# Smaller first units, relays of their own rows, and loads of k, v and x in pieces, in an attention and feed-forward kernel

## The chip, the cores and the metric

One of the eight cores of a Trainium2 chip runs the whole program. A core has TensorE (PE, matrix products into PSUM), VectorE (DVE), ScalarE (ACT), GpSimd (POOL) and SyncE (SP). In this kernel SyncE does nothing but issue the DMA transfers, one after the other in the order of the program; sixteen DMA engines move the bytes. The metric is the device time of one execution in microseconds. The time before is the median of three runs.

## The reference

Four batches of twelve heads, 448 tokens of width 64. The scores of the twelve heads are mixed by a 12 by 12 matrix before the softmax, and the attention weights by another after it. Then comes a block that mixes tokens through rank 32 and channels through a hidden layer of 3072 with relu.

```python
scores = scale * np.matmul(q, k.transpose(0, 1, 3, 2))
scores = np.einsum('bhij,hg->bgij', scores, w_pre)
scores = scores - np.max(scores, axis=-1, keepdims=True)
attn = np.exp(scores)
attn = attn / (np.sum(attn, axis=-1, keepdims=True) + 1e-09)
attn = np.einsum('bhij,hg->bgij', attn, w_post)
x = np.matmul(attn, v)            # then to [B, S, H * D]
...
h = xt @ U @ V                    # xt is x with tokens last
u = x + h.transpose(0, 2, 1)
return u + np.maximum(u @ w_ch1, 0.0) @ w_ch2
```

## The kernel before, in words

The work on attention goes by chunks of ten query tokens: 45 chunks a batch, 180 in all. Chunks are grouped into units, four to a batch: `UNITS` (line 22) gives 12, 12, 12, 9 chunks for batches 0 and 2 and 11, 12, 12, 10 for batches 1 and 3.

For a unit, `load_q` (L384) fetches the query columns and, per batch, `load_k` (L380) the keys in three transfers of one, two and three pairs of heads. For each of the six pairs of heads `qk` (L397) makes scores on TensorE, for all rows of the unit at once, `qk_out` (L401, whose copies stand at L309 and L311) evicts them to a tile s, and two `relay` transfers (L404) carry them, one per head, to a tile t, where the heads lie on partitions, as the mixing needs. A relay moves ten partitions of twelve chunks whatever the unit has. There are two t tiles, used in turn by the units, and three s tiles.

Two chunks make one pair of the softmax part: `premix` (L428) mixes the heads and needs all twelve relays of its units, `neg_max` (L433) is the row maximum on VectorE, `exp` (L438) the exponential on ScalarE, `recip` (L445) and `scale_w` (L449) put the reciprocal of the sum into the second mixing matrix, `postmix` (L461) mixes the heads again on TensorE, and `post_out` evicts into a tile a. When a unit's chunks are done, `av` (L499) multiplies by v in two groups of three pairs of heads, and `store_x` (L508) writes the result to a scratch xs in device memory. `load_v` (L491) fetches the v of a batch in one transfer into a single buffer, so the v of the next batch waits for the last `av` of this one.

After attention, `load_x` (L667) reads a batch of xs back in one transfer into a tile acc; `flip` (L672) transposes, `by_u` (L690) and `by_v` (L703) apply the rank 32 matrices, and `up` (L743), `down` (L763) and `gather` (L767) are the hidden layer. Its weights come as 8-byte words (`load_raw`, L580), are made into floats on VectorE and GpSimd, and each is split into a high and a low part. Eight of these pieces are converted early, between the attention steps, and parked in device memory (L612, L616).

The order of all of this is computed when the program is built. Each step is given with its engine, a guessed cost, a rank, the steps that it needs and the buffers it takes; `Plan.order` plays the engines forward in time and lets each take the ready step of lowest rank whose buffers are free. The program is then written in that order, engine by engine. So the order of the transfers on SyncE is fixed, and a transfer that must wait holds up all behind it. Two lines decide much of it, the rank and cost of a relay and of a load:

```python
plan.add(("relay", u, h), [("SP", (1040, 1000))], partial(relay, u=u, h=h), r + RANK["qo"], [("qk_out", u, p)], [s, ("t", u)])
plan.add(("v", un.b), [("SP", (500, 6700))], partial(load_v, b=un.b), rank_av(u, 0) - RANK["vr"], (), [("vr", un.b)])
```

SyncE's transfers take eight completion semaphores in turn, DMAHW0 to DMAHW7 in the order, so a transfer waits until the one eight places before it has landed.

Of the kernel before, what the change touches and what calls it, by code (L numbers as in the profile page):

```python
# [21 lines left out]
UNITS = [[12, 12, 12, 9], [11, 12, 12, 10]] * 2  # L22
NG = 4
NJ = 4
# [19 lines left out]
class Unit:  # L44


    def __init__(self, b, gi):
        self.b, self.gi, self.n = b, gi, UNITS[b][gi]
        self.i0 = MC * sum(UNITS[b][:gi])
        self.rows = MC * self.n  # L50
        self.tokens = min(S, self.i0 + self.rows) - self.i0
# [5 lines left out]
    av_step=1.6, post=4.6, kr=6, vr=4, qr=9.129, mx=0.782, ex=1.2, ep=2.4, po=0.9, qo=0.4, rl=10.285,  # L57
# [202 lines left out]
def build(tc, q2, kt, vj, wpre_in, wpost_in, u_in, v_in, ident, w1j, w2, out, show=None):  # L260
# [5 lines left out]
    def pool(ctx, name, bufs, side="left", **kw):  # L266
# [4 lines left out]
        wr=3, e=3, st=4, a0=1, a1=1, a2=1, vr=1, x=2, kr=2, k=2, q=3, s=3, tmp1=1,  # L271
# [75 lines left out]
    units = [Unit(b, gi) for b in range(B) for gi in range(NG)]  # L347
# [34 lines left out]
    def load_q(eng, u, p, n, src):  # L382
        q = tile_of(("q", u), lambda: sb["q"].tile([128, H // 2, QW], F32, "q"))
        eng.dma_start(out=q[:, p:p + n], in_=src[:, p:p + n])  # L384
# [14 lines left out]
    def qk_out(eng, u, p):  # L399
        s = T["s", u, p] = sb["s"].tile([QW, 2, S], F32, "s")  # L400
        copy(eng, s, T.pop(("qk", u, p))[:QW, :, :S])  # L401

    def relay(eng, u, h):
        eng.dma_start(out=tt[u % 2][QA + h::H], in_=T["s", u, h // 2][QA:, h % 2])  # L404

    at = 0
    for u, un in enumerate(units):
        b, size = un.b, 128 * (H // 2) * QW
        src = q2[at:at + size].rearrange("(p h i) -> p h i", p=128, h=H // 2)
        at += size  # L410
        for p in range(0, H // 2, 3):
            plan.add(("q", u, p), [("SP", (430, 880))], partial(load_q, u=u, p=p, n=3, src=src), rank_qk(u, 2 * p) - RANK["qr"], (), [("q", u)])
        for p in range(H // 2):
            r = rank_qk(u, 2 * p)
            o, s = ("qk", (u, p)), ("s", (u, p))
            plan.add(("qk", u, p), [("PE", 760)], partial(qk, u=u, p=p), r, [("q", u, p // 3 * 3), ("k", b, (0, 1, 1, 3, 3, 3)[p])],
                     [o, ("q", u), ("k", b)])
            plan.add(("qk_out", u, p), OUT(2 * S), partial(qk_out, u=u, p=p), r + RANK["qo"], [("qk", u, p)], [o, s], port=())
            for h in (2 * p, 2 * p + 1):
                plan.add(("relay", u, h), [("SP", (1040, 1000))], partial(relay, u=u, h=h), r + RANK["qo"], [("qk_out", u, p)], [s, ("t", u)])  # L420
# [68 lines left out]
    def load_v(eng, b):  # L489
        v = T["v", b] = sb["vr"].tile([AP, H // 2, 2, NJ, D], F32, "v")  # L490
        eng.dma_start(out=v, in_=vj[b].rearrange("p (h i n d) -> p h i n d", h=H // 2, i=2, n=NJ))  # L491

    def av(eng, u, p):
        v, a, n = T["v", units[u].b], T["a", u], units[u].rows
        z = T["z", u, p] = bank("av", (u, p))[:, :AV * 120].rearrange("p (a n) -> p a n", a=AV)
        for c in range(AV):
            for jj in range(NJ):
                for i in range(2):
                    eng.matmul(z[i * D:(i + 1) * D, c, :n], lhsT=v[:, p + c, i, jj, :], rhs=a[:, jj * H + 2 * (p + c) + i, :n], start=(jj == 0), stop=(jj == NJ - 1))  # L499
# [10 lines left out]
    for u, un in enumerate(units):  # L510
        if un.gi == 0:
            plan.add(("v", un.b), [("SP", (500, 6700))], partial(load_v, b=un.b), rank_av(u, 0) - RANK["vr"], (), [("vr", un.b)])
        for p in range(0, H // 2, AV):
            r = rank_av(u, p)
            z, x = ("av", (u, p)), ("x", u)
            plan.add(("av", u, p), [("PE", 300 + AV * 816)], partial(av, u=u, p=p), r, [("v", un.b)] + [("post_out", c) for c in range(first[u], first[u + 1]) if ("post_out", c) in plan.steps],
                     [("vr", un.b), (f"a{u % 3}", u), z])
# [148 lines left out]
    def load_x(eng, b):  # L666
        eng.dma_start(out=acc[b], in_=xs[b].rearrange("c p s -> p c s"))  # L667
# [213 lines left out]
```

## Time and profile before

| | |
|---|---|
| median of 3 runs | 1167.31 us (1164.23 to 1170.02) |
| the profiled execution | 1160.33 us |
| its span in the profile | 1158.2 us, mean granted TensorE clock 0.979 |
| TensorE busy | 1086.0 us, 94% |
| VectorE, ScalarE, GpSimd busy | 730.3, 390.5 and 258.4 us |
| moved by DMA | 118.18 MB, mean 102 GB/s |
| attention, by the last postmix | up to about 380 us |

The profile page gives the busy time of each engine, the span in 40 slices with the granted clock (1.00 is full speed, 0.50 half) and the DMA rate, the chain of work that ended last, and the costliest groups of instructions. The trace behind it answers for single stretches, lines and tiles. Names such as t<-s mean "written from". TensorE's weight loads are a row of their own, PEld.

### The profile page before, as it was taken

Reading aid. Unit: us, or ns where it says so; the run is one execution under the profiler, and the core shown is the slowest. Engines: PE = TensorE matmul, PEld = TensorE weight load, DVE = VectorE, ACT = ScalarE, POOL = GpSimd, SP = SyncE. Lnnn points to the kernel's source line nnn. Section 1 sums busy time; section 2 is a strip of 40 time slices with the busy share of each in tenths; the row PEclk is TensorE's granted clock in tenths of the full one; section 3 lists DMA queues with packets and bytes.
Section 4 is the critical chain, followed back from the end, with each engine's and each line's share of the span. In section 5 each row is a group of like instructions: output and inputs, shape, how many; then the busy total and the mean of one; then the engine's idle time right before and its main releaser. Section 6 shows DMA issues by size and latency. Waiting matters only on the chain.

```text
span 1158.2 us, 29292 instructions
## 1 busy us (share of the span) xinstructions
PE 1086.0 (94%) x12456; PEld 902.0 (78%) x12456; DVE 730.3 (63%) x1271; ACT 390.5 (34%) x817; POOL 258.4 (22%) x389
## 2 busy tenths in 40 slices
PE   3799898989989879999999999999999999999998
PEld 0476565656657768898898989898989898989897
DVE  0554454545766775887676767676767676776634
ACT  2677565757666523322111111111111121212100
POOL 3111111111123332243122222221222222222100
PEclk7899999999999889999999999999999999999999
DMA  8556746656775710122111111111111121112004
GB/s 239 188 178 189 202 154 189 173 172 183 205 212 180 224 43 1 28 69 69 54 55 55 55 55 55 55 55 55 55 55 55 55 55 56 55 41 60 10 14 178
DMA packets 68030, 118.18 MB, mean 102 GB/s; under 512 B 17804, under 2 KB 54108, under 8 KB 67420
## 3 DMA queue, kind: packets, MB, share of 16 engines
q1 hardware_dynamic: 67900, 116.31, 33.9%
q8 instruction: 98, 1.61, 0.6%
q14 instruction: 32, 0.26, 0.1%
HBM read 62.72 MB, written 12.28 MB: 65 GB/s over the span
## 4 chain that ended last, share of the span: by engine, by line
PE 83%; DMA 7%; DVE 5%; issue 2%; ACT 2%; SPq 1%; POOL 0%; ACTq 0%; DVEq 0%; POOLq 0%
PE bank L743 30%; PE bank L763 29%; PE bank L461 6%; PE bank L499 6%; DMA t<-s 5%; PE bank L428 5%; PE bank L397 5%; PE bank L690 1%; DVE acc L767 1%; DMA v<-in_vj 1%; PE bank L672 1%; SPq L404 1%; DVE xl L316 1%; ACT s L309 1%; DVE a L599 1%
## 5 line engine op out<-in xcount | busy, mean ns | idle before, releaser
L767 DVE TENSOR_TENSOR acc<-acc,bank 128x448 f32<-128x448 f32 x300 | 183.9, 619 | 76.2 <-PE bank L763 71.2
L763 PE MATMUL bank<-hh,w1l 128*128 128x448 f32 x576 | 215.2, 374 | 1.7 <-DVE xl L316 0.6
L743 PE MATMUL bank<-uh,w0l 128*128 128x448 f32 x576 | 213.0, 370 | 0.9 <-DVE acc L706 0.7
L743 PE MATMUL bank<-ul,w0h 128*128 128x448 f32 x576 | 212.5, 369 | 0.0
L743 PE MATMUL bank<-uh,w0h 128*128 128x448 f32 x576 | 212.3, 369 | 0.0
L763 PE MATMUL bank<-hl,w1h 128*128 128x448 f32 x576 | 211.4, 367 | 0.0
L763 PE MATMUL bank<-hh,w1h 128*128 128x448 f32 x576 | 211.4, 367 | 0.0
L748 ACT ACTIVATE hh<-bank 128x448 fp32r<-128x448 f32 x96 | 52.3, 545 | 396.2 <-PE bank L743 364.1
L433 DVE TENSOR_REDUCE mx<-bank 128x2 f32<-128x896 f32 x90 | 97.7, 1087 | 109.7 <-PE bank L428 109.7
L608 POOL TENSOR_TENSOR a<-a,x 128x384 f32<-128x384 f32 (+2 forms) x99 | 100.2, 1012 | 292.1 <-DVE x L604 283.6
L461 PEld LDWEIGHTS bank<-wr,e 60*56 60x56 f32 (+1 forms) x5760 | 103.2, 133 | 57.6 <-issue 48.2
L752 DVE SCALAR_TENSOR_TENSOR hl<-bank,hh 128x448 fp32r<-128x448 f32 x96 | 59.8, 623 | 133.2 <-ACT hh L748 132.1
L763 PEld LDWEIGHTS bank<-hh,w1l 128*128 128x128 f32 x576 | 108.3, 188 | 22.0 <-DVE acc L767 9.7
L461 PE MATMUL bank<-wr,e 60*56 60x60 f32 (+1 forms) x5760 | 107.9, 220 | 16.8 <-issue 13.6
L397 PE MATMUL bank<-k,q 64*60 64x448 f32 (+1 forms) x768 | 101.0, 580 | 20.8 <-ACT s L309 13.6
L438 ACT ACTIVATE e<-bank,mx 128x448 f32<-128x448 f32 x180 | 112.7, 636 | 16.3 <-DVE rc L445 8.5
L743 PEld LDWEIGHTS bank<-uh,w0l 128*128 128x128 f32 x576 | 109.1, 189 | 11.6 <-DVE acc L706 1.0
L743 PEld LDWEIGHTS bank<-uh,w0h 128*128 128x128 f32 x576 | 108.9, 189 | 10.1
L743 PEld LDWEIGHTS bank<-ul,w0h 128*128 128x128 f32 x576 | 108.9, 189 | 9.9
L763 PEld LDWEIGHTS bank<-hh,w1h 128*128 128x128 f32 x576 | 108.3, 188 | 9.7
L763 PEld LDWEIGHTS bank<-hl,w1h 128*128 128x128 f32 x576 | 108.3, 188 | 9.0
L428 PE MATMUL bank<-t,wpre 64*64 64x448 f32 x720 | 92.8, 560 | 8.3 <-DMA t<-s 4.8
(59 smaller groups left out, 1147.3 us busy)
## 6 DMA issues: line engine op xcount, KB each, us to landing
t<-s SPq DMA_DIRECT2D x192, 210.0 KB
kr<-in_w1j SPq DMA_DIRECT2D x48, 384.0 KB
kr<-in_w SPq DMA_DIRECT2D x48, 384.0 KB
q<-in_q SPq DMA_DIRECT2D x32, 186.0 KB
v<-in_vj SPq DMA_DIRECT2D x4, 1440.0 KB
acc<-xs SPq DMA_DIRECT2D x4, 1344.0 KB
out<-acc SPq DMA_DIRECT2D x24, 224.0 KB
xs<-x SPq DMA_DIRECT2D x10, 360.0 KB
```

What stands on the lines that cost most here:

```text
L397: eng.matmul(o[at, i, :S], lhsT=q[d, p, at], rhs=k[d, p, :], start=True, stop=True)
L428: eng.matmul(o[64 * j:64 * j + 64, i, :S], lhsT=wpre[64 * i:min(64 * i + 64, QW)], rhs=tt[u % 2][64 * i:min(64 * i + 64, QW), n, :], start ...
L433: eng.tensor_reduce(out=mx, in_=T["pre", k][:, :, :S], axis=AX.X, op=ALU.max, negate=True)
L438: eng.activation(out=e[:, i], in_=T["pre", k][:, i, :S], func=ACTF.Exp, bias=T["mx", k][:, i:i + 1], accum_out=sm[:, i:i + 1])
L461: eng.matmul(d[:, jj * H:(jj + 1) * H, i], lhsT=e[64 * j:64 * j + HALF, i, j0:j0 + m], rhs=wr[64 * j:64 * j + HALF, i].rearrange("p (g m) ...
L499: eng.matmul(z[i * D:(i + 1) * D, c, :n], lhsT=v[:, p + c, i, jj, :], rhs=a[:, jj * H + 2 * (p + c) + i, :n], start=(jj == 0), stop=(jj == ...
L608: eng.tensor_tensor(out=f32(a), in0=f32(a), in1=f32(x), op=ALU.add)
L743: eng.matmul(ps, lhsT=w[:, c * 128:(c + 1) * 128], rhs=u[:, c, :], start=(i == 0), stop=(i == 3 * KC - 1))
L748: eng.activation(out=hh, in_=T["up", f, b], func=ACTF.Relu)
L752: eng.scalar_tensor_tensor(out=hl, in0=T.pop(("up", f, b)), scalar=0.0, in1=f32(T["hh", f, b]), op0=ALU.max, op1=ALU.subtract)
L763: eng.matmul(ps, lhsT=w[:, cut], rhs=h, start=(i == 0), stop=(i == len(todo) - 1))
L767: eng.tensor_tensor(out=dst, in0=dst, in1=T.pop(("dn", f, b, c)), op=ALU.add)
```

## The change

The first batch has five units instead of four, of 4, 8, 10, 12 and 11 chunks; batch 1 keeps 11, 12, 12, 10, batch 2 has 12, 12, 12, 9 and batch 3 has 11, 12, 12, 10, as before. A unit's q, its QK products, evictions and relays cover only the unit's own rows (`wide`). The k of a batch comes in six transfers of one pair of heads, v in six of one pair into three buffers of half a batch each, and x in six of one chunk of 128 channels. A `gate` ties k, q and v loads to a premix, so that the planner can't place them earlier, and the q of units 1 to 3 to a relay. There are four s tiles instead of three. The host packs q to match, and a scratch size for DMAs of GpSimd is set smaller, which leaves more on-chip memory.

```diff
-UNITS = [[12, 12, 12, 9], [11, 12, 12, 10]] * 2
+UNITS = [[4, 8, 10, 12, 11], [11, 12, 12, 10], [12, 12, 12, 9], [11, 12, 12, 10]]
...
+        self.wide = QA + self.rows
...
-    av_step=1.6, post=4.6, kr=6, vr=4, ...
+    av_step=1.6, post=4.6, kr=6, vr=2, vl=1.5, kl=2, ...
...
-        wr=3, e=3, st=4, a0=1, a1=1, a2=1, vr=1, x=2, kr=2, k=2, q=3, s=3, tmp1=1,
+        wr=3, e=3, st=4, a0=1, a1=1, a2=1, vr=3, x=2, kr=2, k=2, q=3, s=4, tmp1=1,
...
     def rank_qk(u, h):
-        if u == 0:
-            return RANK["k0"] + h * RANK["kstep"]
+        if u < 2:
+            return (20 * u - 40) + 0.7 * h
         return first[u] - RANK["qk_lead"] - (11 - h) * RANK["qk_step"]
+
+    def gate(c):
+        return [("premix", min(int(c), NC - 1) // 2)] if c >= 0 else []
...
     for b in range(B):
-        for p, n in ((0, 1), (1, 2), (3, 3)):
-            plan.add(("k", b, p), [("SP", (450, 1050 * n))], partial(load_k, b=b, p=p, n=n), rank_qk(b * NG, 2 * p) - RANK["kr"], (), [("k", b)])
+        for p in range(H // 2):
+            r = rank_qk(lead[b], 2 * p) - RANK["kr"] - (RANK["kl"] * (6 - p) if b else 0)
+            plan.add(("k", b, p), [("SP", (450, 1050))], partial(load_k, b=b, p=p, n=1), r, gate(r) if b else (), [("k", b)])
...
-            at = slice(64 * j, min(64 * j + 64, QW))
+            at = slice(64 * j, min(64 * j + 64, units[u].wide))
+            if at.start >= at.stop:
+                continue
...
     def relay(eng, u, h):
-        eng.dma_start(out=tt[u % 2][QA + h::H], in_=T["s", u, h // 2][QA:, h % 2])
+        un = units[u]
+        eng.dma_start(out=tt[u % 2][QA + h::H, :un.n], in_=T["s", u, h // 2][QA:un.wide, h % 2])
...
-                plan.add(("relay", u, h), [("SP", (1040, 1000))], ...
+                plan.add(("relay", u, h), [("SP", (140 + 75 * un.n, 85 * un.n))], ...
...
-    def load_v(eng, b):
-        v = T["v", b] = sb["vr"].tile([AP, H // 2, 2, NJ, D], F32, "v")
-        eng.dma_start(out=v, in_=vj[b].rearrange("p (h i n d) -> p h i n d", h=H // 2, i=2, n=NJ))
+    def load_v(eng, b, p):
+        v = tile_of(("v", b, p // AV), lambda: sb["vr"].tile([AP, AV, 2, NJ, D], F32, "v"))
+        eng.dma_start(out=v[:, p % AV], in_=vj[b].rearrange("p (h i n d) -> p h i n d", h=H // 2, i=2, n=NJ)[:, p])
...
-            plan.add(("v", un.b), [("SP", (500, 6700))], partial(load_v, b=un.b), rank_av(u, 0) - RANK["vr"], (), [("vr", un.b)])
+            for p in range(H // 2):
+                r = rank_av(u, 0) - RANK["vr"] - RANK["vl"] * (6 - p)
+                plan.add(("v", un.b, p), [("SP", (460, 1150))], partial(load_v, b=un.b, p=p), r, gate(r), [("vr", (un.b, p // AV))])
...
-    def load_x(eng, b):
-        eng.dma_start(out=acc[b], in_=xs[b].rearrange("c p s -> p c s"))
+    def load_x(eng, b, c):
+        eng.dma_start(out=acc[b][:, c, :], in_=xs[b][c])
```

Two places of SyncE's order show what moves. The first is its start, before: the rows between the first k of batch 0 and the first relays.

```order
L380 DMA k_123<-in_kt 128x1344
L357 DMA wpost_116<-in_wpost 128x60
L384 DMA q_130<-in_q 128x372 x2
L384 DMA q_133<-in_q 128x372 x2
L491 DMA v_140<-in_vj 120x3072
L380 DMA k_142<-in_kt 128x448
L380 DMA k_142<-in_kt 128x896
L380 DMA k_142<-in_kt 128x1344
L404 DMA t_1_114<-s_146 10x12x448 x2
```

The same place now, from the last k of batch 0 to the first relay of unit 1 (a row with x2 is two transfers).

```order
L384 DMA k_119<-in_kt 128x448 x2
L358 DMA wpre_113<-in_wpre 124x64
L358 DMA wpost_116<-in_wpost 128x60
L501 DMA v_134<-in_vj 120x512 x2
L413 DMA t_1_114<-s_139 10x4x448 x2
...
L413 DMA t_1_114<-s_154 10x4x448 x2
L388 DMA q_165<-in_q 128x3x84 x2
L413 DMA t_1_114<-s_167 10x4x448 x2
L413 DMA t_1_114<-s_170 10x4x448 x2
L388 DMA q_186<-in_q 128x3x104 x2
L413 DMA t_2_115<-s_184 10x8x448 x2
```

The q of units 1 and 2, all of v and the k of batch 1 stood ahead of the first relay; now only two pieces of v do, and the relays have 4 chunks instead of 12.

The second place is where batch 0 gives way to batch 1, before, with what each transfer waits for: the load of v and the relays behind it.

```order
L491 DMA v_1905<-in_vj 120x3072 [waits DMAHW1_49,PE_49]
L508 DMA xs_1_109<-x_1814 128x6x88 [waits DMAHW2_49,Activation_49]
L404 DMA t_1_114<-s_1890 10x12x448 [waits DMAHW3_49,DVE_49,PE_49]
L404 DMA t_1_114<-s_1890 10x12x448 [waits DMAHW4_49]
L404 DMA t_1_114<-s_1954 10x12x448 [waits DMAHW5_49,DVE_49]
```

And now:

```order
L501 DMA v_1908<-in_vj 120x512 [waits DMAHW2_49]
L413 DMA t_1_114<-s_1827 10x12x448 [waits DMAHW3_49,Activation_49]
L413 DMA t_1_114<-s_1827 10x12x448 [waits DMAHW4_49]
L501 DMA v_1908<-in_vj 120x512 [waits DMAHW5_49]
L501 DMA v_1908<-in_vj 120x512 [waits DMAHW6_49]
L501 DMA v_1987<-in_vj 120x512 [waits DMAHW7_49,PE_49]
L518 DMA xs_1_109<-x_1906 128x6x108 [waits DMAHW0_49,Activation_49]
L501 DMA v_1987<-in_vj 120x512 [waits DMAHW1_49]
L413 DMA t_2_115<-s_2005 10x12x448 [waits DMAHW2_49,PE_49,Activation_49]
```

One v of 120 by 3072 floats has become six of 120 by 512 among the relays, and the wait for TensorE to be done with the old v stands at the fourth of them.

## Rows read from the trace of the kernel before

**Rows 1.** Busy time by stage: us, busy (instructions) of each engine, granted clock, DMA share, GB/s.

```profile
0.00:36.00 36.00, 12.70 (x84) 3.46 (x88) 0.00 (x0) 9.40 (x11) 9.28 (x6) 0.78 0.78 233
36.00:58.00 22.00, 20.18 (x506) 11.07 (x505) 15.21 (x20) 15.16 (x36) 3.66 (x13) 0.89 0.58 182
100.00:380.00 280.00, 255.09 (x6998) 178.12 (x7002) 158.11 (x247) 184.42 (x404) 51.50 (x155) 0.98 0.62 184
380.00:440.00 60.00, 46.80 (x349) 41.37 (x339) 46.27 (x82) 22.98 (x47) 20.59 (x21) 0.86 0.40 117
500.00:1158.00 658.00, 653.79 (x3155) 589.45 (x3153) 443.76 (x809) 111.34 (x222) 152.26 (x155) 1.00 0.19 58
```

**Rows 2.** The chain that ended at 60 us, in order of time: start us, us, what.

```profile
13.14 14.36 DMA t<-s
27.60 0.91 ACT s L309
...
35.72 3.27 PE bank L428 x16
...
42.28 1.09 PE bank L461 x53
```

**Rows 3.** SyncE's timeline at the start: start us, us, line, transfer.

```profile
6.91 0.35 SPq L491 DMA_DIRECT2D v<-in_vj  x1
7.41 2.97 SPq L380 DMA_DIRECT2D k<-in_kt  x3
```

**Rows 4.** TensorE's waits up to 400 us: total us, times, longest.

```profile
PE bank L461 <- issue: 13.6, 9, 4.9
...
PE bank L499 <- issue: 3.8, 3, 2.3
```

**Rows 5.** TensorE's timeline, single rows behind a gap (idle before, releaser in brackets).

```profile
140.71 1.00 PE L461 MATMUL bank<-wr,e 60*64 60x60 f32 x28 [4.89 <-issue]
...
184.59 0.63 PE L499 MATMUL bank<-a,v 120*64 120x120 f32 x8 [2.34 <-issue]
...
234.89 1.59 PE L461 MATMUL bank<-wr,e 60*64 60x60 f32 x62 [3.03 <-issue]
```

**Rows 6.** SyncE's timeline, the later loads of v, and k of batch 3.

```profile
130.95 0.36 SPq L491 DMA_DIRECT2D v<-in_vj  x1
...
176.35 1.37 SPq L380 DMA_DIRECT2D k<-in_kt  x3
...
224.43 0.36 SPq L491 DMA_DIRECT2D v<-in_vj  x1
...
312.81 0.38 SPq L491 DMA_DIRECT2D v<-in_vj  x1
```

**Rows 7.** DMA queue in 131 to 141 us: packets, MB, share of 16 engines.

```profile
q1 hardware_dynamic: 1008, 1.91, 85.5%
```

**Rows 8.** Busy time after the two long gaps, columns as in Rows 1.

```profile
140.00:147.00 7.00, 6.29 (x119) 4.53 (x118) 2.32 (x3) 0.42 (x1) 0.39 (x1) 0.54 0.59 196
235.00:239.00 4.00, 4.00 (x79) 2.06 (x79) 0.00 (x0) 2.20 (x5) 0.06 (x1) 0.57 0.68 241
```

**Rows 9.** Line 404, the relays on SyncE: duration ns min/median/max, first and last start.

```profile
L404 SPq DMA_DIRECT2D t<-s x192: 755/756/1621, 10.5 to 353.2; - x192
```

**Rows 10.** The chain, single pieces of QK (one pair) and AV.

```profile
58.93 0.75 PE bank L397 x8
...
79.50 2.61 PE bank L499 x48
...
123.37 2.01 PE bank L499 x48
```

**Rows 11.** SyncE's waits up to 400 us: total us, times, longest.

```profile
SPq L404 <- DMA v<-in_vj: 14.2, 4, 6.2
...
SPq L491 <- PE bank L499: 7.4, 2, 4.5
```

**Rows 12.** TensorE's waits from 380 to 500 us.

```profile
PE bank L690 <- DVE xl L316: 9.5, 5, 2.9
```

More of the change, by code (lines that the diff above doesn't have):

```diff
@@ L345, in OUT_A @@
         return [("ACT", 237 + 0.833 * n), ("DVE", 168 + 1.042 * n)]
-    units = [Unit(b, gi) for b in range(B) for gi in range(NG)]
+    units = [Unit(b, gi) for b in range(B) for gi in range(len(UNITS[b]))]
+    lead = [next(u for u, un in enumerate(units) if un.b == b) for b in range(B)]
     nu = len(units)
@@ L411, in build @@
         for p in range(0, H // 2, 3):
-            plan.add(("q", u, p), [("SP", (430, 880))], partial(load_q, u=u, p=p, n=3, src=src), rank_qk(u, 2 * p) - RANK["qr"], (), [("q", u)])
+            r = rank_qk(u, 2 * p) - (RANK["qr"] if u > 1 else 5)
+            plan.add(("q", u, p), [("SP", (430, 880 * un.wide // QW))], partial(load_q, u=u, p=p, n=3, src=src), r, gate(r) + ([("relay",) + ((0, 1), (0, 11), (1, 11))[u - 1]] if 0 < u < 4 else []), [("q", u)])
         for p in range(H // 2):
@@ L515, in build @@
             z, x = ("av", (u, p)), ("x", u)
-            plan.add(("av", u, p), [("PE", 300 + AV * 816)], partial(av, u=u, p=p), r, [("v", un.b)] + [("post_out", c) for c in range(first[u], first[u + 1]) if ("post_out", c) in plan.steps],
-                     [("vr", un.b), (f"a{u % 3}", u), z])
+            plan.add(("av", u, p), [("PE", 300 + AV * 816)], partial(av, u=u, p=p), r, [("v", un.b, p + c) for c in range(AV)] + [("post_out", c) for c in range(first[u], first[u + 1]) if ("post_out", c) in plan.steps],
+                     [("vr", (un.b, p // AV)), (f"a{u % 3}", u), z])
             plan.add(("av_out", u, p), OUT(AV * un.rows), partial(av_out, u=u, p=p), r + 0.65 * AV, [("av", u, p)], [z, x], port=())
@@ L715, in build @@
         RB = RL + RANK["rb0"] if b == 0 else NC + RANK["rb1"] + RANK["rbs"] * b
-        plan.add(("x", b), [("SP", (480, 6300))], partial(load_x, b=b), RB - RANK["x0"], [("first", "mid", "third", "third")[b]] + [("xs", b * NG + gi) for gi in range(NG)])
         for c in range(KC):
@@ L719, in build @@
             tp, hp, xn = ("lr", ("tp", b, c)), ("lr", ("hp", b, c)), ("xn", (b, k))
-            plan.add(("tp", b, c), [("PE", 440)], partial(flip, b=b, c=c), r, ["ident", ("x", b)], [tp, xn])
+            plan.add(("x", b, c), [("SP", (480, 1050))], partial(load_x, b=b, c=c), r - RANK["x0"],
+                     [("first", "mid", "third", "third")[b]] + [("xs", u) for u in range(nu) if units[u].b == b])
+            plan.add(("tp", b, c), [("PE", 440)], partial(flip, b=b, c=c), r, ["ident", ("x", b, c)], [tp, xn])
             plan.add(("xh", b, c), [("ACT", 593)], partial(flip_h, b=b, c=c), r, [("tp", b, c)], [tp, xn])
@@ L827, in lay_out @@
     for b in range(B):
-        for gi in range(NG):
+        for gi in range(len(UNITS[b])):
             un = Unit(b, gi)
-            part = np.zeros((2, D, H // 2, QW), q.dtype)
+            part = np.zeros((2, D, H // 2, un.wide), q.dtype)
             for n in range(un.n):
```

24 lines of the change are left out of this document (12 added, 12 removed).

## Prediction

> **What bounds the kernel now.** I read the table by stage first [rows 1]. Up to 36 us TensorE is busy for 12.7 us, from 36 to 58 for 20.2 of 22, from 100 to 380 it idles 24.9 us of 280, from 380 to 440 it idles 13.2, and after 500 only 4.2 of 658. So the feed-forward part moves as a block with whatever lets the attention part end sooner, and three places can give time: the start, the gaps in 100 to 380, and the passage at 380 to 440.
>
> *Start.* The chain of waits [rows 2] shows what the first premix, at 35.72, waits for: relays (t<-s), the longest piece 14.36 us. They are late because of what stands ahead of them in SyncE's queue [rows 3]: v of batch 0 and k of batch 1 go out before the first relay. By the shapes in the order, at 4 bytes: k twice 1344 KB, six loads of q of 186, v 1440, wpre and wpost 61, and unit 0's twelve relays of 210 make 7825 KB, 8.01 MB. The stage up to 36 us moved 233 GB/s [rows 1]; at that rate 8.01 MB take 34.4 us, and the premix came 1.3 us later. **The start is the queue's bytes.**
>
> *Gaps.* Of TensorE's waits up to 400 us [rows 4], 13.6 and 3.8 us are put down to "issue", a wait for nothing that the profile shows: 17.4 of the 26.7 us idle in the stages 36 to 58 and 100 to 380. Of the single gaps [rows 5], 4.89 us ends at 140.71 and 3.03 us at 234.89, each behind a v load (issued at 130.95 and 224.43); 2.34 us ends at 184.59, behind the three k loads from 176.35 [rows 6]. From 131 to 141 us that v and the relays behind it held the DMA engines for 85.5% [rows 7]. After the two long gaps the granted clock fell [rows 8]: 0.54 of full in 140 to 147, 0.57 in 235 to 239, so mostly 1.2 instead of 2.4 GHz. I read these gaps as TensorE's instructions arriving late while the DMA engines hold a deep queue. By the order's waits SyncE lets a transfer go when the eighth before it is done, so eight are in flight: a v of 1440 KB with seven relays of 210 is 2.9 MB, eight relays are 1.7.
>
> A rule speaks against that reading, in the Trainium skill, "Runtime: NRT & Kernel Launch", section "Instruction fetch mechanics": instructions come in 16 KiB blocks over the sequencer's own DMA queue, and the cost of crossing into a new block is mostly hidden. By it the gaps have another cause and smaller v loads buy nothing; the trace has the two longest gaps right behind v, so it agrees only in part, and that is rival 1.
>
> **The change, part by part.**
>
> *First units.* By the order, 3109 KB now stand up to unit 0's last relay: k 1344, q of unit 0 132 (44 columns instead of 124), two pieces of v 480, q of unit 1 252, wpre and wpost 61, and twelve relays of 70 (4 chunks instead of 12). At 233 GB/s that is 13.7 us, plus the same 1.3: 15.0 at best. The last relay also needs the last k, a QK product, an eviction of 0.91 [rows 2], a free s buffer and an issue of 0.76 [rows 9]; with 7 us for that the worst is 22. I take 18, nearer the bytes, because they explained the start before. First premix: from 35.7 to 18.
>
> That isn't 18 us of gain, because units 1 to 3 must still be fetched. At 233 GB/s: unit 1 (q of unit 2 312 KB, relays 1680) 8.8 us, ready at 26.8; unit 2 (q 372, v 960, relays 2100) 15.1, at 41.8; unit 3 (relays 2520, k 224, q 342, a store 120) 14.1, at 55.9. From 18 to 55.9 I count TensorE at 37.9 us less 5 of idling (3.5 before unit 1: about 8.6 us of work stand ready for these 8.8, but from premix to postmix takes 6.6 [rows 2]; 1.5 before unit 2) and less 2 for a low clock: 31 us of work, with 3.8 done before 18 (QK of unit 0, which is half, and two pairs of unit 1, at 0.75 a pair [rows 10]). Before, by 55.9: 20.2 us from 35.7, less 1.8 idle and some 2 for the clock (0.89 in 36 to 58 [rows 1]), 16.4, and ten QK pairs done ahead, 7.5. So 34.8 against 23.9: 10.9 us ahead. Of this the added work comes off: half a unit of QK (three pairs, 2.25 us) and one more unit's fixed part of AV, two groups of 0.2 (48 matmuls take 2.61 us at 120 rows and 2.01 at 90 [rows 10], which leaves 0.2 at none). **Start: −8 us.** Ends: −14 (premix at 15, no idling) and −3 (premix at 22).
>
> *v and k in pieces.* No load of k or v is larger than 240 KB, and eight of them are 1.9 MB. The three gaps are 10.3 us; the low clock cost 2.9 (6.29 busy at 0.54) and 1.7 (4.00 at 0.57) [rows 8]: 14.9 us. The other 7.1 us of issue gaps stand next to relays and stay. Because a fourth s buffer lets more relays queue up, I give some back: **−12 us.** Ends: −17 (some of the others go too) and +4 (more of them come).
>
> *v's third buffer.* SyncE waited 14.2 us for places that v held and 7.4 us for AV to free v's buffer [rows 11]. Most of it goes, but TensorE had other pairs to work on (255 of 280 us busy [rows 1]). Nothing; ends −2 and 0.
>
> *More DMAs.* Twelve more relays at 0.755 us [rows 9], 12 more k, 20 more v and 20 more x loads at some 0.43 (0.36 for v, three k in 1.37 [rows 6]): 9.1 + 22.4 = 31.5 us of SyncE over 380, of which 192 relays took 145 before; there is room. Nothing on the path; if that cover is gone, see rival 3. The relays move 38.7 MB instead of 41.3, in a stage where the DMA engines are 0.62 busy [rows 1]: nothing after the start. Six more evictions of 0.91 on ScalarE, busy 184 of 280 us, cost nothing either; late next would be the s buffers. The scratch size concerns DMAs issued by GpSimd, and there are none.
>
> *x in pieces.* Transposes may start when one of six chunks has landed. But from 380 to 500 TensorE waits 9.5 us for xl, a product of VectorE [rows 12], which is busy 46.3 of 60 us in the passage [rows 1]. Nothing; ends −4 (it waited for x behind that) and +4 (20 more issues delay the last x).
>
> **Sum.** −8 −12 = −20. The profiled execution took 1160.33 us, so 1140.3. It lies 7.0 under the median of the runs, 1167.31; on that scale, **1147 us**.
>
> **Rivals.**
>
> 1. *The gaps don't follow v.* They are instruction supply in dense stretches of small matmuls and come elsewhere. For it: the fourth v goes out at 312.81 [rows 6], and none of the longest gaps is behind it. Against: the two longest are behind the second and third. Only the start counts: 1167.3 − 8 = 1159 us.
>
> 2. *The lead is given back.* Units 1 to 3 come so tightly that TensorE waits for relays from 18 to 56 us at a low clock, and what is left is lost when SyncE's places fill. For it: up to 36 us the clock granted was 0.78 [rows 1], with TensorE idle. Against: after 36 us it hardly waited. Of the 20 us about 2 remain: 1165 us.
>
> 3. *Slower: SyncE's queue.* Each small load takes one of eight places and its issue time, and a relay behind a v piece that waits for AV (up to 4.5 us [rows 11]) delays the next unit. If all 31.5 us come to lie on TensorE's path, against 20 gained: 1167.3 + 11.5 = 1179 us. It decides once more than 20 us of relays' lateness reach TensorE. Against: relays run up to a unit ahead, and a unit is over 20 us of work. The Trainium skill, "DMA: Bandwidth & Descriptors", section "Bandwidth", sides with this rival: batch DMAs to 1 MiB or more, with 138 GB/s at 64 KB against 341 at 1 MB. By these two figures the k and v loads, 11.4 MB, would take up to 49 us longer, an estimate from that page, so 1196 us; the trace doesn't bear it out so far, since the stage up to 36 us moved 233 GB/s with only one load over 700 KB [rows 1, 3].
>
> 4. *More than forecast.* Each end at its best (start −14, gaps −17, passage −4): 1132 us.
>
> **Numbers.** Forecast 0.50, rival 1 0.24, rival 4 0.10, rival 2 0.10, rival 3 0.05, anything else slower 0.01. The range 1131 to 1162 takes in the forecast with its bounds and rivals 1 and 4; the likeliest case alone would be 1137 to 1156. A measurement of this kernel can tell about 0.5%, 5.8 us: faster is below 1161.5, so 0.50 + 0.24 + 0.10 and a little of rival 2, 0.85; same 0.09; slower 0.06.
>
> **What would show it.** First premix between 15 and 22 us, and TensorE busy over 30 us between there and 56. No issue gap over 2 us and no drop of the clock between 100 and 380, the issue gaps under 10 us together. The last postmix some 20 us sooner, a passage as long as before, the time after it unchanged. I would be wrong if the first premix came after 25 us, if gaps of 3 us and more stood behind relays alone, or if TensorE came to wait for t<-s again and again after 60 us.

## The result, and the profile after

The changed kernel takes 1179.53 us, median of 13 runs (1169.61 to 1185.44), against 1162.42 for the kernel before, timed beside it. The ratio is 1.0131 [1.0097, 1.0165]: 17 us slower by the medians, 15 by the ratio, where 20 us faster was forecast. Some executions of some of the kernels below are over 1.5% slower than the fastest of the same kernel; the ratios leave these out, the medians hold them. The profiled execution took 1179.75 us, its span is 1177.9.

The table by stage of the changed kernel, columns as in [rows 1]; the row from 440 us is a stretch that the table of before left out:

```profile
0.00:36.00 36.00, 27.45 (x260) 8.51 (x264) 4.67 (x6) 17.55 (x26) 10.43 (x10) 0.95 0.54 153
100.00:380.00 280.00, 257.32 (x6788) 175.19 (x6782) 160.11 (x249) 179.58 (x400) 50.39 (x153) 0.98 0.62 179
380.00:440.00 60.00, 45.08 (x579) 39.42 (x576) 41.05 (x73) 24.35 (x52) 19.01 (x23) 0.86 0.43 137
440.00:500.00 60.00, 49.64 (x238) 42.17 (x236) 32.28 (x56) 15.90 (x32) 9.45 (x11) 0.87 0.03 7
500.00:1158.00 658.00, 653.63 (x3192) 598.23 (x3191) 455.98 (x830) 115.58 (x231) 160.18 (x163) 1.00 0.19 55
```

Up to 36 us TensorE is busy 27.45 us instead of 12.70: the start did become earlier. From 440 to 500 it idles 10.4 us, at a granted clock of 0.87; before, in the same stretch:

```profile
440.00:500.00 60.00, 56.53 (x302) 50.58 (x301) 44.01 (x79) 17.69 (x36) 13.81 (x14) 1.00 0.08 21
```

The chain at the start, columns as in [rows 2]:

```profile
1.65 4.29 DMA k<-in_kt
...
14.02 2.33 DMA q<-in_q
...
16.49 5.17 PE bank L404 x16
21.66 0.91 PE bank L438 x8
```

The first premix (line 438) comes at 21.66, not 35.72, and it stands behind QK products of the second unit (line 404), whose q was late. TensorE's waits up to 400 us, which answer to [rows 4]:

```profile
PE bank L471 <- issue: 11.2, 10, 3.9
PE bank L404 <- DMA q<-in_q: 8.1, 2, 4.3
PE bank L509 <- issue: 6.2, 3, 3.2
PE bank L404 <- issue: 2.9, 2, 1.5
...
PE bank L438 <- issue: 1.5, 1, 1.5
...
PE bank L438 <- DMA t<-s: 0.9, 1, 0.9
```

The gaps with no releaser did not go: 11.2 + 6.2 + 2.9 + 1.5 = 21.8 us, against 13.6 + 3.8 and 1.3 at QK before. 8.1 us of waiting for q is new; both waits end before the first premix, at 3.76 and 16.49 us. For relays (t<-s) TensorE waits 0.9 us in all. From 380 to 500 us, which answers to [rows 12]:

```profile
PE bank L702 <- DVE xl L316: 15.0, 8, 4.9
PE bank L776 <- DVE acc L780: 3.3, 1, 3.3
```

9.5 us for xl became 15.0, and the DN products (line 776) now wait for a gather. Cut at the same products in both traces (first premix, last AV product, UP group 1 and 19 of 96), the 19.7 us between the two spans fall as follows: start −14.1, first premix to last AV +23.5, from there to the first UP group +0.9, the first eighteen UP groups with all between them +17.4 (178.9 against 161.5), the rest −7.9. The last is the pitch of the feed-forward matmuls, about 202 ns in this execution and 206 in that of before; it isn't shown to be an effect of the change. Most of the +23.5 is work, not waiting. From the first premix to the last AV product (before, then after):

```profile
35.70:389.10 353.40, 324.19 (x8731) 224.30 (x8731) 202.95 (x314) 233.53 (x512) 63.99 (x195) 0.98 0.63 186
21.60:398.50 376.90, 345.14 (x8901) 233.99 (x8899) 205.01 (x316) 239.71 (x522) 64.50 (x196) 0.97 0.62 179
```

TensorE is busy 21.0 us longer and idles 2.6 longer. So two stretches had to be explained: what the attention part paid for its earlier start, and a passage in which the change edits only x's loads.

### The profile page after: what moved, and what is told of

It is laid out like the page before. It is cut to its first block, busy times and chain, and to the rows that moved or that the text cites. A ratio compares the mean times of both kernels' runs of the same rounds, so it can differ in the third digit from the quotient of the medians.

```text
span 1177.9 us, 29658 instructions
## 1 busy us (share of the span) xinstructions
PE 1105.7 (94%) x12576; PEld 916.0 (78%) x12576; DVE 733.8 (62%) x1272; ACT 393.9 (33%) x824; POOL 258.1 (22%) x389
## 4 chain that ended last, share of the span: by engine, by line
PE 87%; DVE 5%; issue 3%; ACT 2%; DMA 2%; SPq 1%; DVEq 0%; POOL 0%; ACTq 0%
PE bank L756 30%; PE bank L776 28%; PE bank L404 7%; PE bank L471 7%; PE bank L509 7%; PE bank L438 6%; PE bank L702 1%; DVE acc L780 1%; DVE xl L316 1%; DMA t<-s 1%; PE bank L684 1%; SPq L413 1%; DVE hl L765 1%; ACT hh L761 1%; DVE acc L718 1%
## 5 line engine op out<-in xcount | busy, mean ns | idle before, releaser
L471 PEld LDWEIGHTS bank<-wr,e 60*64 60x64 f32 (+1 forms) x5760 | 104.1, 134 | 50.9 <-issue 44.1
L404 PE MATMUL bank<-k,q 64*64 64x448 f32 (+6 forms) x792 | 116.1, 566 | 11.9 <-DMA q<-in_q 8.1
L471 PE MATMUL bank<-wr,e 60*56 60x60 f32 (+1 forms) x5760 | 109.7, 221 | 12.3 <-issue 11.2
```

The lines of the kernel that those rows point to most:

```text
L404: eng.matmul(o[at, i, :S], lhsT=q[d, p, at], rhs=k[d, p, :], start=True, stop=True)
L471: eng.matmul(d[:, jj * H:(jj + 1) * H, i], lhsT=e[64 * j:64 * j + HALF, i, j0:j0 + m], rhs=wr[64 * j:64 * j + HALF, i].rearrange("p (g m) ...
```

## Experiments

Each group of runs has the times of the kernel before beside it, on the same chip; the ratios in parentheses are to these. A ratio is uncertain by 0.003 to 0.005, so a difference between two of these runs by some 6 to 7 us.

### Narrow second column groups

A QK product is made of two column groups of its unit, the first 64 wide. Before, the second was always 60. Now each unit brings its own width, so the units of 8 and 9 chunks have 20 and 30. The chain of the changed kernel, one pair is 8 matmuls, the first row is two pairs:

```profile
251.11 3.40 PE bank L404 x16
256.33 1.63 PE bank L404 x8
...
270.96 0.75 PE bank L404 x8
```

The pairs up to 262 us belong to the unit of 9 chunks, the one at 270.96 to a unit of 11, with 50 columns: 1.6 us against 0.75, for less work. By start times the second group of 30 runs after its neighbour, not beside it. In the compiled program the groups of 20 and 30 columns use tiles of 64 by 32 of TensorE, all others tiles of 64 by 64; whether the width or the mixture of tiles does it isn't separated here. The edit:

```diff
+        self.cols = self.wide if self.wide <= 64 else max(self.wide, 104)
...
-            at = slice(64 * j, min(64 * j + 64, units[u].wide))
+            at = slice(64 * j, min(64 * j + 64, units[u].cols))
```

(and the same width in q's load and layout; the plan is untouched).

> The changed kernel in its own order, but the QK products of the units of 8 and 9 chunks are computed over 104 columns again (zeros beyond the unit's own rows), so the second column group of each is 40 wide and not 20 or 30. Theory A (in the changed kernel's trace a QK pair with a group of 30 columns takes 1.73 us, with 40, 50 or 60 about 0.80; a group of 32 columns or fewer does not run beside its neighbours): twelve pairs fall to 0.80, 12 x 0.92 = 11 us of TensorE work go, of which the 5.5 of unit 1 may be partly hidden at the start: 5 to 11 us less than the changed kernel's 1179.5, so 1168 to 1174. Theory B (the loss is SyncE's queue of many small transfers): no change beyond 2 us, since no transfer is taken away.

1172.77 us (ratio 1.0101 [1.0069, 1.0134]), 6.8 under the changed kernel by the medians, 3.5 by the ratios, so as a difference of times it isn't clear of the noise. A pair of the same unit in its chain:

```profile
254.08 0.75 PE bank L405 x8
```

The price of a pair is shown; what it costs in all is less than half of the loss in this order. The limit of 32 columns in the expectation wasn't measured: 30 is slow, 40 is not. From the first to the nineteenth UP group it still took 179.8 us.

### The loads of x, k and v

Three runs undo or do one of these alone. x whole again, in the changed kernel's order:

```diff
-        eng.dma_start(out=acc[b][:, c, :], in_=xs[b][c])
+        if c == 0:
+            eng.dma_start(out=acc[b], in_=xs[b].rearrange("c p s -> p c s"))
```

> The changed kernel in its own order, but the whole x of a batch goes in one transfer at the place of its first piece. Theory B (small x transfers hold SyncE's eight places and delay the passage between attention and feed-forward, which took some 17 us longer to get to the twelfth hidden product): 10 us or more faster than 1179.5, and the first matmul of L776 after 440 us sooner. Theory C (the passage is longer because TensorE and VectorE stand in a new order there and idle at the low clock): within 3 us of 1179.5.

1188.36 us (1.0213 [1.0164, 1.0263]): 9 us slower than the changed kernel. k whole and v in halves from batch 1 on, at the place of the first piece:

```diff
+        elif p == 0:
+            eng.dma_start(out=k, in_=kt[b])
...
+        elif p % AV == 0:
+            eng.dma_start(out=v, in_=src[:, p:p + AV])
```

> The changed kernel in its own order, but from batch 1 on all of k goes at the place of its first piece and each half of v at the place of its first piece (720 KB). The prediction's theory (issue gaps come from large loads in the queue): more issue gaps behind them, 5 to 12 us slower than 1179.5. Theory B (many small transfers cost the time): 5 us or more faster. Neither: within 3 us, if the gaps follow the depth of the queue whatever its pieces.

1187.32 us (1.0212 [1.0162, 1.0263]), 8 us slower. In both, the loss lies ahead of the last AV product: from the first premix to there it is 384.6 and 381.3 us, against 376.9. And the kernel before with x in six pieces, planned anew:

```diff
+    def load_x(eng, b, c):
+        eng.dma_start(out=acc[b][:, c, :], in_=xs[b][c])
...
-            plan.add(("tp", b, c), [("PE", 440)], partial(flip, b=b, c=c), r, ["ident", ("x", b)], [tp, xn])
+            plan.add(("tp", b, c), [("PE", 440)], partial(flip, b=b, c=c), r, ["ident", ("x", b, c)], [tp, xn])
```

> The kernel before with x alone in six transfers a batch; its feed-forward order is that of the kernel before from the first hidden product on. Theory B: the passage is longer, 5 us or more over 1162.4. Theory C: the same time as before within 3 us.

1161.52 us (0.9984 [0.995, 1.0017]): no difference. So x in pieces costs nothing that these runs can tell, and in the changed order the pieces of k, v and x help: there a whole load also comes earlier, at the place of its first piece, so size and place aren't separated. The rival that had the right time, SyncE's queue, is out: it needs over 20 us of late relays at TensorE, and the trace has 0.9; and with fewer transfers the kernel became slower. In both runs with whole loads the first eighteen UP groups took 180 us as well. The loss in the passage isn't made by the size of these loads.

### The dealing of half banks

PSUM stands in the program as four tiles of two banks each. The planner deals banks to steps one by one, as they come free. TensorE's order from the first UP product on is the same in both kernels, but the banks are not, and the order shows waits that hold for a whole tile. In the order of the changed kernel TensorE fills bank3_4 for a by_u product (line 702) and then bank3_4 again, its other half, for the UP product:

```
2175 L702 MATMUL bank3_4_61<-xh_9_6681,u4_2_5902 128x256 [waits Activation_49]
2176 L702 MATMUL bank3_4_61<-xh_9_6681,u4_2_5902 128x256 x3
2177 L756 MATMUL bank3_4_61<-uh_1_6276,w0l_4_6568 128x448
```

In the compiled program the by_u product raises no semaphore of its own; the first that can release its reader is that of the last UP matmul. ScalarE's copy of the by_u product, and VectorE's low part of h some 30 us later, in the timelines of the changed kernel:

```profile
422.68 0.37 ACT L309 CAST t<-bank 128x256 fp32r<-128x256 f32 x1 [2.04 <-PE bank L756]
```

```profile
424.10 0.55 DVE L610 SCALAR_TENSOR_TENSOR a<-kr,a 128x384 int32<-128x384 int32 x1
...
425.82 0.56 DVE L616 SCALAR_TENSOR_TENSOR x<-kr,x 128x384 f32<-128x384 uint32 x1
426.41 1.15 DVE L780 TENSOR_TENSOR acc<-acc,bank 128x448 f32<-128x448 f32 x2
...
454.97 0.62 DVE L765 SCALAR_TENSOR_TENSOR hl<-bank,hh 128x448 fp32r<-128x448 f32 x1 [3.82 <-PE bank L756]
```

The copy reads a product that was done at 419 us, but ScalarE idles 2.04 us until the UP product in the other half is done. The low part of h waits 3.82 us for the whole of the next UP product. In between VectorE comes late to the gathers (line 780), and TensorE stands before its third DN product and then works at the lower clock, 0.57 us a matmul where it had 0.37:

```profile
423.44 0.37 PE L776 MATMUL bank<-hh,w1h 128*128 128x448 f32 x1
427.09 0.74 PE L776 MATMUL bank<-hh,w1l 128*128 128x448 f32 x1 [3.28 <-DVE acc L780]
427.62 0.57 PE L776 MATMUL bank<-hl,w1h 128*128 128x448 f32 x1
```

But the rows also show weight narrowing (lines 606 to 616) ahead of the gathers on VectorE, which could be the cause by itself. The test leaves every engine's order alone and only deals the banks anew from the first UP product on, by a greedy rule: for each new product the free bank whose sibling's steps overlap least with its own in the plan.

```diff
     order = plan.order()
+    rebank(plan, order)
...
+            cost = sum(false_wait(s, t) for t in last[h ^ 1][1][-4:] if len(plan.where[t]) == 1)
+            key = (cost, end)
+            if best is None or key < best[0]:
+                best = (key, h)
```

> The changed kernel with every engine's order untouched; only the PSUM half banks of the single-bank products from the first UP product on are dealt out anew, so that a product does not sit in the other half of a two-bank tile while that tile's first half is still being written or read. Theory 'shared tiles': in the passage the changed kernel stands because reads and writes of the two halves of one tile wait for each other (the third DN product for the gather of the first, 3.3 us; the low part of h for the whole next UP product, 3.8 us), and the clock falls after each. It expects the stretch from the first to the seventh UP group to fall from 83 us to 68 to 73 us, the next twelve groups from 96 to 88 to 91, and the whole to be 14 to 20 us under the changed kernel: 1160 to 1166 us. Rival 'DVE order': the weight narrowing that stands ahead of the gathers on DVE is what delays them, whatever the banks: then the stretch stays at 81 to 84 us and the time at 1177 to 1181.

1153.24 us (0.9892 [0.9853, 0.993]), 26 us under the changed kernel and more than expected. The same two instructions, no longer waiting for the other half, in the timelines of this run:

```profile
425.28 0.37 ACT L347 CAST t<-bank 128x256 fp32r<-128x256 f32 x1 [0.55 <-DVE acc L756]
```

```profile
451.04 0.62 DVE L803 SCALAR_TENSOR_TENSOR hl<-bank,hh 128x448 fp32r<-128x448 f32 x1
```

The first six UP groups took 68.2 us instead of 82.8, the next twelve 87.6 instead of 96.1. TensorE still waited 1.8 us for the first gather, where it had waited 3.3, and worked at the lower clock behind it, so VectorE's order has a share, but a small one: all eighteen groups took 155.9 us here, and 154.0 in the kernel before with the same dealing. The dealing is shown to be the cause of the slower passage. It was bad in the kernel before too:

> The kernel before with its own order and the same new dealing of half banks from the first UP product on. 'Shared tiles' expects little to win where the dealing was lucky already: the stretch from the first to the seventh UP group 67 to 71 us (71.6 before), the time 2 to 8 us under the kernel before: 1154 to 1160 us. 'DVE order' expects no difference: 1160 to 1164.

1145.43 us (0.9861 [0.9818, 0.9904]), 17 us under the kernel before, where 2 to 8 were expected. The first eighteen UP groups went from 161.5 to 154.0 us. After them 48 pairs of successive DN products that stood 30 to 140 ns apart too far are gone, some 5 us. That makes 12 or 13 of the 17. In the two profiled executions the pitch of the later feed-forward matmuls also went from 205 to 203 ns, some 6 us; whether the dealing does that isn't shown. With both mends:

> The changed kernel with both mends: QK products of the units of 8 and 9 chunks over 104 columns, and the new dealing of half banks. If the two causes add up, 7 us less than the run with the new dealing alone: 1153 to 1159 us, which is 3 to 9 us under the kernel before. If the narrow products' time is hidden once the passage runs well, as the run with the dealing alone: 1160 to 1166.

1139.94 us (0.9798 [0.9756, 0.9839]): 13 us under the run with the dealing alone by the medians, 11 by the ratios, where 7 were expected. They add up, and the time lies below the range given because the dealing had already brought more than was expected of it.

### What the first units and the pieces are worth

With the two mends in place the parts of the change can be weighed. First the new units with large loads of k, v and x and one buffer for v instead of three, planned anew:

```diff
-        for p in range(H // 2):
+        for p, n in ((0, 1), (1, 2), (3, 3)):
...
-            for p in range(H // 2):
-                r = rank_av(u, 0) - RANK["vr"] - RANK["vl"] * (6 - p)
+            r = rank_av(u, 0) - RANK["vr"] - RANK["vl"] * 3
```

> Only the new first units with relays of their own rows: k, v and x in loads as large as before, planned anew, with QK over 104 columns at least and the new dealing of half banks. If loads in pieces are worth something in a plan made for them, this is 3 to 9 us slower than the run with both mends, 1158 to 1166 us, with the difference between the first premix and the last AV product. If they are worth nothing once the plan knows the loads are large, it is within 2 us of it; and if the many small transfers cost, it is faster by 3 us or more: 1148 to 1154 us.

The ratio is 1.0012 [0.9969, 1.0055]. Against 0.9798 the pieces and the buffers together are worth about 2%, some 25 us, more than expected. The run doesn't separate k, v, x and v's buffers, and its trace isn't read. Then the pieces and the relays of own rows with the old units:

```diff
-UNITS = [[4, 8, 10, 12, 11], [11, 12, 12, 10], [12, 12, 12, 9], [11, 12, 12, 10]]
+UNITS = [[12, 12, 12, 9], [11, 12, 12, 10]] * 2
```

(with the ranks of q and QK as they were before).

> The run with both mends, but with the units of the kernel before (12, 12, 12, 9 and 11, 12, 12, 10 twice): k, v and x in pieces, relays of own rows, no new first units; planned anew. First premix at 33 to 36 us. Theory 'the lead is mostly given back': 1137 to 1144 us, within 4 us of the run with both mends (1139.9), since the 14 us won at the start are eaten by the extra unit and by waits behind it. Rival 'the first units carry the change': 1148 to 1156 us, later by the 10 to 14 us that the first premix is later.

1134.43 us (0.9737 [0.9693, 0.978]). This is the fastest version that does all the work, 28 us under the kernel before. **The first units, for which the plan was made, bring nothing:** the run without them is 5.5 us faster by the medians and 7 by the ratios, which is at the edge of what these runs can tell. The first premix comes at 28.6 us here and at 19.9 with the new units, but from there to the last AV product it is 346.8 us against 370.2. Those 23.4 us are 11.2 of work at full clock (busy time less half of what was at the lower clock), 6.2 of idling, and 6.1 for the lower clock (half of 20.9 − 8.7 us). The work is the seventeenth unit and QK products that were done before the first premix and now stand behind it. At the last AV product the run with the old units is 14.7 us ahead; it gives back 9.7 in a passage that its plan laid otherwise, 163.5 us for the first eighteen UP groups against 153.7.

Units that need no padding:

```diff
-UNITS = [[4, 8, 10, 12, 11], [11, 12, 12, 10], [12, 12, 12, 9], [11, 12, 12, 10]]
+UNITS = [[4, 6, 12, 12, 11], [11, 12, 12, 10], [11, 12, 12, 10], [11, 12, 12, 10]]
```

> The changed kernel with the new dealing of half banks and units of 4, 6, 12, 12, 11 and three times 11, 12, 12, 10, so that no QK product has a second column group narrower than 40 and no padding is needed. If narrow groups are the whole of what separates the run with the new dealing (1153) from the run with both mends (1140): 1136 to 1143 us. If padding did something else too, such as another number of columns for DVE and ACT to copy: 1145 to 1153.

1141.37 us (0.9824 [0.9779, 0.987]): as with padding. As far as these runs can tell, the narrow groups are the whole of that part.

### Gaps without a releaser, and the second q

Both mends, but no loads of k and v after batch 0:

```diff
+        if b:
+            T["k", b] = T["k", 0]
+            return
```

(and the same for v).

> The run with both mends without the loads of k and v after the first batch (the later batches use the first batch's k and v, so that their QK and AV products are of other data; their number and shape stay): 36 loads of 210 to 240 KB fewer between 90 and 320 us, everything else in the same order. If PE's gaps without a releaser between 60 and 390 us (about 18 us of them) come from transfers in front of the instruction supply, they fall to under 8 us and the time to 1126 to 1132 us. If they belong to the dense stretches of small products themselves, they stay at 14 us or more and the time is 1136 to 1141.

1125.26 us (0.9677 [0.9641, 0.9713]), 14.7 us less. The expectation spoke of 60 to 390 us, where the loads had been. TensorE's waits without a releaser there, of the run with both mends (lines 443, 477, 510, 548) and of this one (446, 513, 554):

```profile
PE bank L510 <- issue: 6.6, 7, 2.8
PE bank L548 <- issue: 5.8, 4, 2.6
...
PE bank L477 <- issue: 1.5, 1, 1.5
...
PE bank L443 <- issue: 1.3, 1, 1.3
```

```profile
PE bank L513 <- issue: 5.4, 6, 2.1
PE bank L446 <- issue: 1.3, 1, 1.3
...
PE bank L554 <- issue: 1.0, 2, 0.6
```

15.2 us became 7.7, under the 8 of the first theory, and the time lies just below its range. So about half of these gaps goes with the loads and half stays. Each number is of one execution, and the next run, a near twin of the run with both mends, has 20.0 in the same stretch, so the sizes aren't firm. The rest of the 14.7 us lies in the clock (20.9 us at the lower one became 13.3) and in other waits.

What TensorE waits for in such a gap stands in the DMA records. Besides the program's transfers they hold packets of 16 KB on a queue of their own, q8, of the kind instruction: 99 in the changed kernel, for 25411 instructions of TensorE. In the changed kernel's two longest gaps, those that end at 243.75 and 333.30 us, such a packet starts at 241.16 and at 330.58 and takes 1.21 and 1.25 us. The first is the only one in 235 to 244 us; the row of that queue (packets, MB, share of 16 engines' time):

```profile
q8 instruction: 1, 0.02, 0.8%
```

TensorE goes on 1.37 and 1.47 us after the packet's end. All twelve gaps of over 0.6 us without a releaser that this kernel has up to 400 us end so, 1.2 to 1.6 us after such a packet, and so do all nine of the kernel before (the share of the time that lies 1.15 to 1.65 us behind a packet is 0.10). So the gaps are waits for TensorE's own instructions. Why a packet comes late isn't shown beyond the half that goes with the loads.

Last, the second unit's q ahead of all relays:

```diff
-            r = rank_qk(u, 2 * p) - (RANK["qr"] if u > 1 else 5)
+            r = rank_qk(u, 2 * p) - (RANK["qr"] if u > 1 else 5 if u == 0 else 22)
...
```

(and its ties to a premix and to a relay are dropped).

> The run with both mends with the second unit's q ahead of all relays on SyncE, planned anew: PE's wait of 4.5 us for it at 16 us goes. If a start that is earlier reaches the end, the first premix is at 16 to 18 us and the time 3 to 5 us under the run with both mends: 1135 to 1137. If the lead is given back behind the start whatever its size, the time stays at 1138 to 1143.

1137.94 us (0.9792 [0.9758, 0.9826]), no difference that these runs can tell. TensorE's waits in it:

```profile
PE bank L477 <- DMA t<-s: 6.2, 2, 5.0
PE bank L443 <- DMA q<-in_q: 3.8, 1, 3.8
```

The wait for q went from 8.7 to 3.8 us, and one for relays came in its place; the first premix was at 21.7. The start wasn't made earlier, so whether an earlier one would have reached the end was not tested by this run.

## Why the prediction was wrong

**The bridge.** One part at a time, by the ratios, of 1162 us: banks dealt anew 0.9861 (−16); pieces, own-row relays, buffers and padding 0.9737 (−14); the new first units 0.9798 (+7); padding away 0.9892 (+11); the dealing away 1.0131 (+28). By the medians the steps are −17.0, −11.0, +5.5, +13.3 and +26.3. Each is uncertain by 5 to 7 us, and another order gives other shares: the narrow groups cost 3.5 us with the bad dealing and 11 with the good one, the pieces −14 with the old units and −25 with the new. So of the 15 us of the ratio, −14 is what the change was good for, +7 its first units, 4 to 11 the narrow groups, and 12 to 19 that its dealing happened to be worse than the old one (28 − 16, or, on the way over the padded run, 35 − 16, where 35 is 1.0101 less 0.9798). The forecast also stood on a median of three runs, 1167.3 us; over 13 it is 1162.4, so 5 us of the time forecast were noise of the time before.

*First units: −8.* The premix at 18 came at 21.6, inside the bounds of 15 to 22. TensorE was busy 30.83 us from 21.6 to 56, as the prediction's test asked. That sign came true and proves little, since some 4 us of that time are what four narrow QK pairs cost more than wide ones. The step that failed is the added work, put at 2.65 us. QK up to 400 us, before (L397) and after (L404): busy us of TensorE and of its weight loads, granted clock, DMA share, GB/s:

```profile
0.00:400.00 400.00, 101.02 (x768) 27.22 (x768) 0.96 0.65 191
0.00:400.00 400.00, 116.11 (x792) 29.66 (x792) 0.97 0.62 178
```

That is 15.1 us more, and AV went from 81.5 to 86.1: 19.7 us in all, not 2.65, a little of it from the lower clock. With padding QK takes 106.5 us: about 10 of its 15 are the narrow groups, which the prediction put at nothing. The other 5 are unit 0, "QK of unit 0, which is half": its pairs have one column group of 44 and take as long as pairs of two groups side by side (four matmuls of unit 0, then eight of a unit of 11 chunks):

```profile
11.29 0.91 PE L404 MATMUL bank<-k,q 64*44 64x448 f32 x4
```

```profile
270.73 0.99 PE L404 MATMUL bank<-k,q 64*50 64x448 f32 x8
```

So the lead of 14 us at the first premix was gone by the sixth, and at the seventh the kernel was 6.6 us behind (50.9 us before, 57.5 after): by then TensorE had done 160 QK matmuls and 96 of AV, against 112 and none before. Some of that was work done ahead: at the 46th premix of 90 it is 5.7 us in front again, and at the last 8.4 behind. Idling was not the fault: from 21.6 to 56 us it came to 3.6 us, where 5 were allowed. AV's added work was undersized too: the 48 matmuls of a unit of 4 chunks take 0.70 + 1.02 = 1.72 us by the chain, not the 1.0 that the line through [rows 10] gives at 40 columns, and 1.81 at 80:

```profile
54.20 0.70 PE bank L509 x19
56.56 1.02 PE bank L509 x29
63.29 1.81 PE bank L509 x48
```

With everything else mended, the term was +5.5 to +7. Rival 2, the lead given back, has the outcome but not the mechanism: it had TensorE wait for relays, and the waits for t<-s are 0.9 us.

*v and k in pieces: −12.* The size was nearly right, −11 to −14 with own-row relays and all, and +8 when k and v were made whole again in the changed kernel; but that is luck, since the gaps did not go. With the old units and the new dealing the waits without a releaser up to 400 us are 16.7 us with the pieces and 16.9 without. In the changed kernel the two long gaps behind v went, and others of 3 us and more came, behind relays and small loads. The prediction had named gaps behind relays alone as its refutation; the second, with one load of q among the relays, comes near to that:

```profile
243.75 1.16 PE L509 MATMUL bank<-a,v 120*64 120x120 f32 x9 [3.25 <-issue]
...
333.30 1.15 PE L471 MATMUL bank<-wr,e 60*56 60x60 f32 x33 [3.87 <-issue]
```

```profile
227.66 4.91 SPq L413 DMA_DIRECT2D t<-s  x6
232.61 0.59 SPq L384 DMA_DIRECT2D k<-in_kt  x1
...
322.61 4.76 SPq L413 DMA_DIRECT2D t<-s  x4
327.61 0.40 SPq L388 DMA_DIRECT2D q<-in_q  x1
328.52 2.75 SPq L413 DMA_DIRECT2D t<-s  x2
```

The clock fell after them as before, to 0.62 and 0.57, answering to [rows 8]:

```profile
242.00:251.00 9.00, 7.25 (x99) 3.48 (x100) 0.74 (x1) 1.36 (x2) 0.00 (x0) 0.62 0.35 99
331.00:339.00 8.00, 5.70 (x127) 4.50 (x127) 2.32 (x3) 4.24 (x10) 0.19 (x1) 0.57 0.71 209
```

So "No issue gap over 2 us" failed. The prediction's reading that TensorE's instructions arrive late is borne out by the instruction packets, and so is rival 1, which says the same of the cause; that the large load of v is what makes them late is not. Loads have a part in it, about half of the gaps when all of k and v is left out, but making them small didn't remove it, and the gain of the pieces lies elsewhere. In the run with pieces and old units against the kernel before, both with the new dealing, the profiled executions show −6.5 at the start and −4.9 from the first premix to the last AV product, with 8.7 us at the lower clock instead of 14.6; these are single executions, 4.9 us apart in all.

*More DMAs: nothing; x in pieces: nothing.* Nothing speaks against these. x alone came to −0.9 us, inside its interval. The loads of k and v as such aren't free, 14.7 us in the run that leaves them out, but that run doesn't separate their number from their bytes. Rival 3 gave 1179 us and the kernel took 1179.5, but by another mechanism: TensorE waited 0.9 us for relays, not over 20, and fewer, larger and earlier transfers made the kernel slower by 8 and 9 us. That its number came is a coincidence, and the 49 us more that it estimates for small loads did not show in any run.

*"A passage as long as before."* This step failed by 17.4 us and turned the sign; dealing the banks anew took 23.0 off the same stretch. TensorE's order there is the same in both kernels; what differs, and what the prediction left out, is which half bank each product got, and which engine then waits for whom. The 9.5 us for xl [rows 12] had been a warning that VectorE sits on the path there, so that a late VectorE stops TensorE: the 3.28 us at 427.09 were paid in full, and again at the lower clock behind them. The prediction's costs for the passage, −4 to +4, came from x alone.

*The chances.* 0.06 for slower was too little for a change that makes a planner choose everything anew: none of the four rivals was about the parts of the program that the diff doesn't touch. The wrong sign has two causes, the added work and the dealing, and the prediction put the first at 2.65 us and the second at nothing.

## What to carry to other kernels

When a planner or an allocator decides order and memory, compare all that it decided, also behind the place of the change: buffer and bank numbers per instruction, and who waits for whom, not only the sequence on the busiest engine. Let a tile be what its dependencies need: where waits hold for a whole tile, as in this program, a reader of one product in it waits for the writer of the other. An earlier start is worth something only if the same work stands behind it; count the work that was done before the first product of the next stage, not the time of that product. And price work by a measured piece of its own shape: half the columns were not half the time here, and narrower was slower.

## What the runs showed of the hardware

- Two column groups of a QK product run side by side with a second group of 40, 50 or 60 columns (0.75 to 0.80 us for 8 matmuls) and not with 20 or 30 (1.6 to 1.7 us). Where between 30 and 40 it turns wasn't measured. One group of 44 alone takes as long as two side by side (0.91 us for 4 matmuls, 0.99 for 8, ends included).
- AV's 48 matmuls take 1.72 us at 40 columns, 1.81 at 80, then 2.01 at 90 and 2.61 at 120 [rows 10]: at 80 columns and fewer a matmul of this shape takes 36 to 38 ns.
- The stall of 3.28 us that ended at 427.09 cost more than itself: the next DN matmuls, up to 430.24, took 0.57 us apiece instead of 0.37, with starts 0.37 us apart instead of 0.20.
- TensorE's gaps without a releaser ended 1.2 to 1.6 us after a 16 KB packet of the instruction queue had landed, in 21 of 21 cases of the two kernels. Without 36 loads of 224 and 240 KB they fell from 15.2 to 7.7 us between 60 and 390 us.
- The pitch of the same feed-forward matmuls was 205 ns with the dealing of the kernel before (two profiled executions), 202 to 204 with that of the changed kernel (four), and 203 with the new dealing (seven of eight; 206.5 in the other), some 6 to 12 us over the rest of the span; no run here explains it.
